# A float32 causal mask inside the score products, second weights moved by 32 to 96 bytes, and a new instruction order, in a fused attention and two-expert kernel

## The chip, the cores and the metric

The kernel runs on one core of a Trainium2 chip. The metric is device time in microseconds (us) of one execution; several executions are made and the median counts. Engines are called as in the profile: PE is the matrix engine (PEld its weight loads), DVE, ACT and POOL are the vector, scalar and GpSimd engines, SP issues the DMAs.

## The reference, cut to what matters

```python
scores = scale * np.matmul(q, k.transpose(0, 1, 3, 2))          # 4 x 8 heads, 576 x 576, depth 64
cum = np.cumsum(np.maximum(s, 0.0), axis=-1)
bias = -(cum[:, :, :, None] - cum[:, :, None, :])
scores = np.where(causal, -1000000000.0, scores + np.minimum(bias, 0.0))
attn = np.exp(scores - scores.max(-1, keepdims=True))
attn = attn / (attn.sum(-1, keepdims=True) + 1e-09)
x = (attn @ v), heads side by side                               # 2304 tokens x 512
h = x @ w_in;  x = (h - np.tanh(h)) @ w_out                      # expert 1: 512 -> 2048 -> 512
h = x @ w2_in; solu = h * softmax(h)                             # expert 2: 512 -> 1024 -> 512
out = (layer_norm(solu) * g_ln) @ w2_out
```

## The kernel before

**Attention.** Two heads make a pair (16 pairs). A unit is one block of 64 queries of a pair against all keys up to it. A score step on PE (`scores`, line 573) takes one or two units. Its products (line 631) are float32, 64 x 64 weights (the queries) with 64 to 512 keys streamed, and each is put in one of the four 64 x 64 parts of the array, so that two heads, or two heads of two units, run side by side. Behind them, one for each unit, stands `bar` (line 637): a bfloat16 product over the whole 128 x 128 array, identity `idb` times `mask`, that adds -8e9 to the masked corner, 64 columns wide, on top of the scores in PSUM. `soften` on DVE (line 646) and ACT (line 657) makes the exponentials, POOL or DVE divides (line 661), PE turns the result by transposes (line 695) over the whole array, and `weigh` (line 734) multiplies by the values in 128 x 64 parts.

**Expert 1.** Tokens come in 9 blocks of 256. For each of the 16 slices of 128 hidden columns (f) there are 12 products into the hidden layer (`h_part`, line 781) and 12 back (`x2_part`, line 804), all 128 x 128 weights and 256 columns, on inputs split into a high and a low float32r part (weights `ih`, `il`, `oh`, `ol`). The first 8 slices ("first weights", tiles `wih0` to `wol0`, pool `wa`) are used from within the attention on; the last 8 ("second weights", `wih8` to `wol8`, pool `wb`) can be converted when the attention's buffers are closed, and are used after the first ones. Each half has 9 x 8 x 24 = 1728 products.

**Expert 2** follows block by block: products of 512 columns (lines 895, 959), softmax and norm on ACT and DVE, transposes (line 945). Its 16 weight pieces (`load_w2`) go into the place of the first weights after `switch`.

**Weight conversion.** `split_w` loads each piece by SP and rebuilds it by a chain of DVE operations (lines 371, 374, 377, 382), a high part (line 263) and a low part (line 287).

**Addresses.** In the program before, the allocator puts the first weights at 50656, 67040, 83424 and 99808 bytes of a partition, which are all 96 modulo 128. The three pads of 32 bytes in `w1_tiles` put the second ones at 137088, 153504, 169920 and 186336: 0, 32, 64 and 96 modulo 128. Expert 2's weights stand where the first ones stood, and the streamed tiles `xb` and `gh` at 32 modulo 128.

**Order.** Nothing is ordered by hand: `Plan.order` simulates the engines with cost functions (`t_mm`, `t_score`, ...), takes at each turn the step that can start first (within `LOOK` ns of an engine's clock the one of lowest `prio`), and writes the instructions of all engines in that order. The priorities are sums of the constants in `T`, several per job, weight piece (`W`, `U`) and block (`V`, `B`, `E`). Where the plan sees PE idle early on, it puts in filler products (line 477).

Of the kernel before, what the change touches and what calls it, by code (L numbers as in the profile page):

```python
# [8 lines left out]
F32 = mybir.dt.float32  # L9
# [3 lines left out]
BF16 = mybir.dt.bfloat16  # L13
# [5 lines left out]

FAR = 1.0e12  # L20
TICK, DUTY = 10240 / 3, 3060.0
LOOK = {"mode": 0.0, "pe": 11.77, "act": 47.99, "dve": 2.284, "pool": 702.3}

T = dict(sums=40.52, warm=44.7, unit0=-0.03201, unit1=0.08366, pace0=0.04788, pace1=0.3542, pace2=0.1082,
         pace3=13.37, pace4=63.81, lead=-77550000.0, vlead=0.3186, fetch=-45.72, w_at0=-124.0, w_step0=88410000.0,
         w_at1=3074.0, w_step1=1163.0, m_at0=2982000.0, m_step0=502700.0, m_at1=-0.0455, m_step1=980500.0, xp=-0.01,
         m_pace=0.07888, xb=-49220.0, wb=1548.0, wb_step=153700.0, p2=0.0, w2_step=-164.7, block=11790.0,
         E2=1981000.0, e2=1981000.0, e2b=1210.0, p2_pace0=-0.08075, p2_pace=-0.01, rstd=1740.0, done=-7.542,
         J0=-1214.0, J1=123.5, J2=-37230000.0, J3=-79020000.0, J4=-1186.0, J7=-26.54, J9=-3494000000.0,
         J10=-17800000.0, J11=2977.0, J12=3382.0, J13=3590.0, J15=2472000.0, J18=20.95, W0=267800000.0, W1=-121.6,  # L30
         W2=-16950.0, W3=33270000.0, W4=-226.7, W5=-199100.0, W6=2897.0, W7=9934000.0, W9=18630.0, W13=22220.0,
         W14=22.66, W15=281800000.0, U0=-38150000.0, U1=559.7, U2=52.13, U3=-3570000.0, U4=9070.0, U6=32180.0,
         U7=-4163000.0, U9=258000000.0, U10=3425000000.0, U12=10250000000.0, U13=807.0, U14=6095.0,
         U15=12740000000.0, V00=115400.0, V01=-388500.0, V02=-428000.0, V04=1191000.0, V05=109.8, V07=43130.0,
         V08=158600.0, V12=244.3, V13=-36030.0, V14=65320.0, V15=-732.0, V16=519600.0, V17=-761.7, V18=42900000.0,
         B1=5947000000.0, B3=188400000.0, B4=-13420.0, B5=11.83, B6=13110000000.0, B7=26550000.0, B8=-32810.0,
         E0=-1258000000.0, E1=2850000.0, E3=-5713000.0, E4=-644800.0, E5=-1430000.0, E6=2519000.0, E7=-7736.0,
         E8=-1861000000.0, E9=630300000.0, E10=726.4, E11=-2977000.0, E13=-66200.0, E14=-33270.0, E15=-651600000.0,
         E16=206400000.0, E17=17370.0)
CONTEND = True  # L40
LANDING = 2300.0
SWITCH = 95.0
FILL = True
PEN = {"rstd-pool": -6.211e-19, "rstd-dve": 45.24, "copy-act": 2.286e-06, "copy-dve": 2064.0, "copy-pool": 261000.0, "move-act": -109.6, "move-dve": 5.891e-78, "diff-dve": 6.446e-11, "diff-pool": -15.23, "pad-dve": 1.284e-17, "pad-pool": 64710000.0, "norm-dve": 0.04456, "norm-pool": -798.1}

DELAY = {("act", "act"): 0.0, ("act", "dve"): 175.0, ("act", "pe"): 240.0, ("act", "pool"): 165.0,
         ("dve", "act"): 130.0, ("dve", "dve"): 128.0, ("dve", "pe"): 205.0, ("dve", "pool"): 195.0,
# [35 lines left out]
class Plan:  # L83
# [7 lines left out]
    def add(self, ways, deps=(), acq=(), rel=(), prio=0.0, late=0.0):  # L91
        s = Step(ways, deps, acq, rel, round(prio, 2), late)
        s.seq = len(self.steps)
        self.steps.append(s)
        return s

    def order(self):
# [25 lines left out]
        def could(s, w):  # L123
            t = max(clock.get(w[0], T["warm"] if w[0] == "pe" else 560.0), s.when[w[0]])
            return max(t, port) if CONTEND and (w[0] == "pool" or isinstance(w[1], Shared)) else t
# [9 lines left out]
        for _ in range(len(self.steps)):  # L135
            best = None
            for eng, cand in ready.items():
                t0 = clock.get(eng, 560.0)
                t1 = t0 + LOOK.get(eng, 30.0)
                for s, w in cand:  # L140
# [6 lines left out]
                    if t < FAR:  # L147

                        key = (max(t + LOOK["mode"] * (w[0] == "pe" and s.mode[0] != mode), t1), s.prio, s.seq)
                        if best is None or key < best[0]:  # L150
# [40 lines left out]
def own(part):  # L191

    return T.get(part, 0.0)


def t_mm(*parts, slow=1):

    return (sum(k * max(107.0, slow * n / 2.4 + (13.3 if slow == 1 else 2.5)) for n, k in parts),
            sum(k * max(107.0, slow * n / 1.2) for n, k in parts), sum(k * n * max(1, slow // 2) for n, k in parts))


def t_score(n, parts):

    a = t_mm((n, 1), slow=4)
    return a[0] + 45.0 + 30.0 * parts, a[1] + 45.0 + 60.0 * parts, a[2] + 64 * parts


def t_turn(n, k=1):
    return t_mm((n, k), slow=2)
# [19 lines left out]
class Kernel:  # L229
# [70 lines left out]
    def setup(self):  # L300
        tc = self.tc
        e = self.ctx.enter_context
        c = e(tc.tile_pool(name="const", bufs=1, side="left"))
        self.idn = c.tile([128, 128], F32, name="idn")
        self.one = c.tile([128, 1], F32, name="one")
        self.idx = c.tile([128, 128], F32, name="idx")
        self.idb = c.tile([128, 128], BF16, name="idb")
        self.mask = c.tile([128, 64], BF16, name="mask")
        c.tile([128, 56], BF16, name="pad_left")
        self.mo = e(tc.tile_pool(name="mo", bufs=1, side="left"))  # L310
        self.st = e(tc.tile_pool(name="st", bufs=8, side="left"))
        self.dr = e(tc.tile_pool(name="dr", bufs=1, space=DRAM))
        self.cum_d = self.dr.tile([self.NP, 3 * self.S], F32, name="cum_d")
        self.xd = [self.dr.tile([4, 128, 2, self.S], F32, name=f"xd{b}") for b in range(self.B)]
        self.pd = [self.dr.tile([128, 4, TB], F32, name=f"pd{j}") for j in range(self.NB)]
        self.st.tile([128, 16], F32, name="pad_st", bufs=1)
        self.wes = ExitStack()
        self.wa = self.w1_tiles(self.wes.enter_context(tc.tile_pool(name="wa", bufs=1, side="left")), 0, FA)
        self.aes = ExitStack()
        self.ap = self.aes.enter_context(tc.tile_pool(name="att", bufs=1, side="right"))  # L320
        self.cv, self.cvb = self.ap, 1
        self.pes = ExitStack()
        self.px = self.pes.enter_context(tc.tile_pool(name="px", bufs=1, space=PSUM))
        self.ps = self.pes.enter_context(tc.tile_pool(name="pb", bufs=BUFS["ps"], space=PSUM))
# [14 lines left out]
    def w1_tiles(self, pool, f0, nf):  # L339
        d = {"f0": f0, "nf": nf, "ready": {}}  # L340
        d["ih"] = pool.tile([128, 4, nf * 128], F32R, name=f"wih{f0}")
        if f0:
            pool.tile([128, 8], F32, name="pad_il")
        d["il"] = pool.tile([128, 4, nf * 128], F32R, name=f"wil{f0}")
        if f0:
            pool.tile([128, 8], F32, name="pad_oh")
        d["oh"] = pool.tile([128, nf, 512], F32R, name=f"woh{f0}")
        if f0:
            pool.tile([128, 8], F32, name="pad_ol")
        d["ol"] = pool.tile([128, nf, 512], F32R, name=f"wol{f0}")  # L350
        return d

# [76 lines left out]
    def prologue(self):  # L429
        nc, S = self.nc, self.S  # L430
        add = self.add
        V = {}
# [5 lines left out]
        def consts():  # L438
            make_identity(nc, self.idn)
            for h in range(2):  # L440

                nc.gpsimd.tensor_copy(self.idx[:, 64 * h:64 * h + 64], self.idn[:, 64 - 64 * h:128 - 64 * h])
            nc.gpsimd.tensor_copy(self.idb, self.idn)
            nc.gpsimd.memset(self.mask, 0.0)
            for h in range(2):
                m = self.mask[64 * h:64 * h + 64, :]
                nc.gpsimd.affine_select(out=m, in_=m, pattern=[[-1, 64]], compare_op=ALU.is_ge, fill=NEG, base=0,
                                        channel_multiplier=1)
# [17 lines left out]
        s = add("dve", 1040, sums, [l, self.one_ready], acq=("pt1",), rel=("pt1",))  # L466
# [17 lines left out]
    def attention_job(self, jb):  # L484
# [8 lines left out]
        lead = self.lead  # L493
        pre = lead + T["fetch"]

# [70 lines left out]
    def units(self, jb, rows, V, sums):  # L566

        nc, add = self.nc, self.add
# [9 lines left out]
        made, ats = [X for X in (self.unit(jb, i, V, Y, n) for n, i in enumerate(rows))], []  # L578
        last = rows[-1] == self.jobs[jb][2]

        def scores():
# [7 lines left out]
            for X in made:  # L589
                X["bar"]()  # L590

        s = add("pe", t_score(64 * rows[-1], len(rows)), scores, V["made"], acq=("ps",) * sum(len(X["parts"]) for X in made) + ("U",) * len(made),
                rel=("q", "kn") * last)
        s.mode = (2, 0)
        s.after = V["scores"][-1:] + sums
        V["scores"].append(s)
        dones = []
# [16 lines left out]
    def unit(self, jb, i, V, Y, n):  # L614
        nc, add = self.nc, self.add
# [5 lines left out]
        X = {}  # L621

        def parts_of(h):

            return slice(64 * h, 64 * h + 64), slice(64 * (h ^ n), 64 * (h ^ n) + 64)
# [8 lines left out]
        def bar():  # L634

            a, z = X["parts"][-1]
            nc.tensor.matmul(X[a][:, z - 64 - a:z - a], lhsT=self.idb, rhs=self.mask, start=False, stop=True,  # L637
                             skip_group_check=True)

# [496 lines left out]
```

## Time and profile before

| | |
|---|---|
| median of 3 runs | 828.76 us (826.08, 828.76, 830.53) |
| the profiled execution | 825.83 us, of which the span of instructions is 824.0 us |
| PE busy | 807.8 us, 98% of the span |
| DVE, ACT, POOL busy | 517.7, 370.4, 161.0 us |
| granted PE clock, mean of the span | 0.998 |

The profiled execution's 1.8 us outside the span are start and end. Its time lies below all three runs. A busy PE is one with a product under way; products overlap, so the spacing of their starts, not their duration, is what one costs in a row.

### The profile page before, as it was taken

Reading aid. Unit: us, or ns where it says so; the run is one execution under the profiler, and the core shown is the slowest. Engines: PE = TensorE matmul, PEld = TensorE weight load, DVE = VectorE, ACT = ScalarE, POOL = GpSimd, SP = SyncE. Lnnn points to the kernel's source line nnn. Section 1 sums busy time; section 2 is a strip of 40 time slices with the busy share of each in tenths; the row PEclk is TensorE's granted clock in tenths of the full one; section 3 lists DMA queues with packets and bytes.
Section 4 is the critical chain, followed back from the end, with each engine's and each line's share of the span. In section 5 each row is a group of like instructions: output and inputs, shape, how many; then the busy total and the mean of one; then the engine's idle time right before and its main releaser. Section 6 shows DMA issues by size and latency. Waiting matters only on the chain.

```text
span 824.0 us, 16453 instructions
## 1 busy us (share of the span) xinstructions
PE 807.8 (98%) x6176; PEld 692.3 (84%) x6176; DVE 517.7 (63%) x1412; ACT 370.4 (45%) x933; POOL 161.0 (20%) x339
## 2 busy tenths in 40 slices
PE   8898999999999999999899999999999999999998
PEld 5465667677779999999899998899988898999886
DVE  6777877777756887633488877554317374346834
ACT  5686787767774455433245442222222222223312
POOL 2353433333330000000000013130003132020403
PEclk9999999999999999999999999999999999999999
DMA  7996796586437887664665501122100120100001
GB/s 208 266 293 177 205 305 188 176 253 212 142 103 229 278 259 239 196 219 139 219 190 165 159 11 39 52 64 77 53 25 26 39 78 14 39 2 26 25 26 39
DMA packets 89135, 112.40 MB, mean 136 GB/s; under 512 B 10768, under 2 KB 73232, under 8 KB 89056
## 3 DMA queue, kind: packets, MB, share of 16 engines
q1 hardware_dynamic: 89056, 111.35, 44.4%
q8 instruction: 49, 0.80, 0.4%
q14 instruction: 30, 0.25, 0.1%
HBM read 87.63 MB, written 23.70 MB: 135 GB/s over the span
## 4 chain that ended last, share of the span: by engine, by line
PE 85%; DVE 5%; DMA 4%; ACT 3%; issue 1%; POOL 0%; SPq 0%; ACTq 0%; DVEq 0%; POOLq 0%
PE t L781 21%; PE big L895 12%; PE t L959 12%; PE big L804 11%; PE acc L804 10%; PE t L631 6%; PE t L734 6%; PE t L695 5%; PE t L945 2%; ACT U L657 1%; PE t L637 1%; DMA pd<-xp 1%; DVE U L646 1%; DMA cd<-in_moe_w_in_dram 1%; DMA xb<-xd 1%
## 5 line engine op out<-in xcount | busy, mean ns | idle before, releaser
L781 PE MATMUL t<-xb,wih 128*128 128x256 f32 x1152 | 206.8, 282 | 4.3 <-DVE g L790 3.7
L781 PEld LDWEIGHTS t<-xb,wih 128*128 128x128 f32 x1152 | 176.0, 188 | 6.8 <-DVE g L790 5.0
L781 PE MATMUL t<-xb,wil 128*128 128x256 f32 x576 | 160.9, 279 | 1.5 <-DVE wil L287 1.5
L661 POOL TENSOR_SCALAR U<-U,r 128x64 f32<-128x64 f32 (+8 forms) x144 | 85.4, 606 | 153.4 <-DVE r L576 54.4
L781 PEld LDWEIGHTS t<-xb,wil 128*128 128x128 f32 x576 | 108.6, 189 | 1.7 <-DVE wil L287 1.7
L804 PE MATMUL big<-gh,woh 128*128 128x256 f32 x576 | 105.4, 284 | 0.2 <-DVE gh L287 0.2
L804 PE MATMUL acc<-gh,woh 128*128 128x256 f32 x576 | 103.4, 282 | 0.4
L263 ACT CAST gh<-g 128x256 fp32r<-128x256 f32 x142 | 57.2, 405 | 88.0 <-PE big L804 45.7
L804 PEld LDWEIGHTS big<-gh,woh 128*128 128x128 f32 x576 | 89.8, 191 | 1.1 <-DVE gh L287 0.6
L786 ACT ACTIVATE th<-t 128x256 f32<-128x256 f32 x144 | 54.6, 381 | 80.3 <-PE t L781 52.4
L657 ACT ACTIVATE U<-U,m 128x192 f32<-128x192 f32 (+8 forms) x144 | 80.1, 558 | 22.4 <-DVE m L646 19.8
L895 PE MATMUL big<-w2ih,x 128*128 128x512 f32 x288 | 89.5, 392 | 0.0
L804 PEld LDWEIGHTS acc<-gh,woh 128*128 128x128 f32 x576 | 87.3, 188 | 1.4 <-ACT xp L263 0.8
L287 DVE TENSOR_TENSOR gh<-g,gh 128x256 fp32r<-128x256 f32 x129 | 55.8, 435 | 49.7 <-ACT gh L263 48.7
L804 PE MATMUL big<-gh,wol 128*128 128x256 f32 x288 | 81.4, 283 | 0.0
L804 PE MATMUL acc<-gh,wol 128*128 128x256 f32 x288 | 80.1, 278 | 0.0
L790 DVE TENSOR_TENSOR g<-t,th 128x256 f32<-128x256 f32 x144 | 60.2, 419 | 23.1 <-ACT th L786 20.3
L646 DVE CUSTOM_DVE_ANT_0 U<-bc,t 128x192 f32<-128x192 f32 (+8 forms) x144 | 61.3, 446 | 18.8 <-PE t L637 12.8
L631 PE MATMUL t<-kn,q 64*64 64x288 f32 (+8 forms) x640 | 66.1, 425 | 0.3 <-DMA q<-in_q_dram 0.3
L937 POOL TENSOR_SCALAR u<-y,va 128x1 f32<-128x1 f32 x54 | 33.8, 625 | 160.9 <-DVE y L932 157.2
L895 PEld LDWEIGHTS big<-w2ih,x 128*128 128x128 f32 x288 | 52.9, 188 | 10.2
L900 DVE TENSOR_REDUCE m<-big 128x1 f32<-128x1024 f32 x18 | 22.0, 1222 | 60.8 <-PE big L895 60.8
(100 smaller groups left out, 1368.9 us busy)
## 6 DMA issues: line engine op xcount, KB each, us to landing
xb<-xd SPq DMA_DIRECT2D x17, 1024.0 KB, 6.2
cd<-in_moe_w_in_dram SPq DMA_DIRECT2D x24, 512.0 KB, 5.3
cd<-in_moe_w_out_dram SPq DMA_DIRECT2D x24, 512.0 KB, 3.9
bc<-cum_d SPq DMA_DIRECT2D x32, 288.0 KB, 6.5
pd<-xp SPq DMA_DIRECT2D x18, 512.0 KB, 4.2
xp<-pd SPq DMA_DIRECT2D x18, 512.0 KB, 4.5
xd<-xs SPq DMA_DIRECT2D x16, 320.0 KB, 3.8
kn<-in_k_dram SPq DMA_DIRECT2D x16, 288.0 KB, 5.2
```

The lines of the kernel that those rows point to most:

```text
L263: nc.scalar.copy(o, i)
L287: return self.any([("dve", t_dve(n, pair=True), lambda: nc.vector.tensor_tensor(*views(), op), "diff-dve"), ("pool", t_pool(n), lambda: nc ...
L631: nc.tensor.matmul(X[a][c, :z - a], lhsT=V["q"][r, o:o + 64], rhs=V["k"][r, a:z], start=True, stop=True, skip_group_check=True)
L646: nc.vector.tensor_tensor_reduce(out=X["u"][:, a:z], in0=V["bc"][:, n, a:z], in1=X[b][:, a - b:z - b], scale=-0.125, scalar=X["m"] if "m" ...
L657: nc.scalar.activation(out=X["u"][:, :nk], in_=X["u"][:, :nk], func=AF.Exp, scale=-1.0, bias=X["m"], accum_out=Y["s"][:, n:n + 1])
L661: eng.tensor_scalar(X["u"][:, :nk], X["u"][:, :nk], Y["r"][:, n:n + 1], 1.0, ALU.mult, ALU.mult)
L781: nc.tensor.matmul(ps, lhsT=w[l][:, k, f * 128:f * 128 + 128], rhs=xb[:, r, k, :], start=k == 0 and x == 0, stop=k == 3 and x == 2)
L786: nc.scalar.activation(out=X["th", f], in_=X["h", f], func=AF.Tanh)
L790: nc.vector.tensor_tensor(X["g", f], X["h", f], X["th", f], ALU.subtract)
L804: nc.tensor.matmul(X["acc"][:, m, :], lhsT=w[l][:, f, m * 128:m * 128 + 128], rhs=X["gh", f][:, r, :], start=f == c0 and m % 2 == 0 and x ...
L895: nc.tensor.matmul(X["h"][:, n, :], lhsT=self.x2[j][:, l, k, 128 * o:128 * o + 128], rhs=r[:, k, 512 * n:512 * n + 512], start=k == 0 and ...
L959: nc.tensor.matmul(X["po"], lhsT=X["lt", k // 4][:, l, k % 4, :], rhs=r[:, k, :], start=k == 0 and a == 0, stop=k == 7 and a == 2)
```

## The change

The mask becomes float32 (`mask` 128 x 64 float32, `idb` gone, the pad beside it 240 instead of 112 bytes: 496 bytes in all before and after, so nothing behind them on that side moves). `bar` becomes two plain float32 products for each unit, 64 x 64 weights out of the float32 identity, in the same two parts of the array as the unit's scores. The three pads between the second weights' tiles go, so that all four lie at the remainder of the last one. The cost functions say so (`t_score`: 64 more columns, and a score step ends in the mode of 64 x 64 parts; `t_mm`: 11.5 instead of 13.3 ns over the streaming of a product). All constants `LOOK`, `T` and `PEN` are new, and with them the order on every engine. The diff, with the constants cut to those of the second weights and the expert 2 pieces:

```diff
-LOOK = {"mode": 0.0, "pe": 11.77, "act": 47.99, "dve": 2.284, "pool": 702.3}
+LOOK = {"mode": 0.0, "pe": 0.0, "act": 4.357, "dve": 110.5, "pool": 55.88}
...
-  wb=1548.0, wb_step=153700.0, p2=0.0, w2_step=-164.7, block=11790.0,
-  U0=-38150000.0, U1=559.7, U2=52.13, U3=-3570000.0, U4=9070.0, U6=32180.0, U7=-4163000.0, U9=258000000.0,
-  U10=3425000000.0, U12=10250000000.0, U13=807.0, U14=6095.0, U15=12740000000.0,
+  wb=-399.9, wb_step=-100.3, p2=-472600.0, w2_step=-0.01596, block=0.02797, B0=112600.0,
+  U1=19.08, U2=18.21, U4=236600.0, U5=-10090.0, U6=-462000.0, U7=-567700000.0, U8=847800000.0, U9=-7644000.0,
+  U10=1000000000.0, U11=-163400000.0, U14=2981000.0,
...
-    return (sum(k * max(107.0, slow * n / 2.4 + (13.3 if slow == 1 else 2.5)) for n, k in parts),
+    return (sum(k * max(107.0, slow * n / 2.4 + (11.5 if slow == 1 else 2.5)) for n, k in parts),
...
-def t_score(n, parts):
-    a = t_mm((n, 1), slow=4)
-    return a[0] + 45.0 + 30.0 * parts, a[1] + 45.0 + 60.0 * parts, a[2] + 64 * parts
+def t_score(n):
+    a = t_mm((n + 64, 1), slow=4)
+    return a[0] - 45.0, a[1] - 90.0, a[2]
...
-        self.idb = c.tile([128, 128], BF16, name="idb")
-        self.mask = c.tile([128, 64], BF16, name="mask")
-        c.tile([128, 56], BF16, name="pad_left")
+        self.mask = c.tile([128, 64], F32, name="mask")
+        c.tile([128, 60], F32, name="pad_left")
...
-        if f0:
-            pool.tile([128, 8], F32, name="pad_il")
         d["il"] = pool.tile([128, 4, nf * 128], F32R, name=f"wil{f0}")
-        if f0:
-            pool.tile([128, 8], F32, name="pad_oh")
         d["oh"] = pool.tile([128, nf, 512], F32R, name=f"woh{f0}")
-        if f0:
-            pool.tile([128, 8], F32, name="pad_ol")
         d["ol"] = pool.tile([128, nf, 512], F32R, name=f"wol{f0}")
...
-            nc.gpsimd.tensor_copy(self.idb, self.idn)
...
-        s.mode = (2, 0)
+        s.mode = (2, 2)
...
-            nc.tensor.matmul(X[a][:, z - 64 - a:z - a], lhsT=self.idb, rhs=self.mask, start=False, stop=True,
-                             skip_group_check=True)
+            for h in range(2):
+                r, c = parts_of(h)
+                nc.tensor.matmul(X[a][c, z - 64 - a:z - a], lhsT=self.idn[r, r], rhs=self.mask[r], start=False, stop=True,
+                                 skip_group_check=True)
```

## Rows read from the trace of the kernel before

**Rows 1.** The page, busy time, share of the span and instructions of each engine.

```profile
PE 807.8 (98%) x6176; PEld 692.3 (84%) x6176; DVE 517.7 (63%) x1412; ACT 370.4 (45%) x933; POOL 161.0 (20%) x339
```

**Rows 2.** The page, the chain that ended last, shares of the span by engine.

```profile
PE 85%; DVE 5%; DMA 4%; ACT 3%; issue 1%; POOL 0%; SPq 0%; ACTq 0%; DVEq 0%; POOLq 0%
```

**Rows 3.** Busy time by stage: stretch, its us, busy us (instructions), granted clock, DMA.

```profile
0.00:40.00 40.00, 34.37 (x274) 19.66 (x276) 27.91 (x131) 23.62 (x76) 12.12 (x33) 1.00 0.88 233
...
395.00:440.00 45.00, 41.52 (x332) 40.70 (x331) 31.24 (x65) 19.23 (x44) 0.00 (x0) 0.96 0.63 196
...
760.00:824.00 64.00, 60.27 (x286) 49.78 (x284) 34.26 (x63) 15.56 (x25) 15.62 (x45) 1.00 0.08 29
```

**Rows 4.** The chain in order of time: start us, us, what; long uninterrupted stretches.

```profile
317.91 9.89 PE t L781 x84
...
352.87 9.53 PE t L781 x84
...
574.39 11.30 PE t L781 x96
...
585.70 11.39 PE big L804 x96
...
755.78 10.89 PE big L895 x48
```

**Rows 5.** Timeline of PE where the second weights begin (line 804 first, 781 second).

```profile
394.90 0.39 PE L804 MATMUL acc<-gh,woh 128*128 128x256 f32 x2
395.12 0.28 PE L804 MATMUL acc<-gh,wol 128*128 128x256 f32 x1
395.24 0.39 PE L781 MATMUL t<-xb,wih 128*128 128x256 f32 x2
395.47 0.28 PE L781 MATMUL t<-xb,wil 128*128 128x256 f32 x1
395.59 0.40 PE L781 MATMUL t<-xb,wih 128*128 128x256 f32 x2
```

**Rows 6.** Groups of PE by line and shape: busy us, mean ns, idle before.

```profile
L637 PE MATMUL t<-mask,idb 128*128 128x64 bf16 x144 | 19.5, 199 | 0.0
```

**Rows 7.** Timeline of PE, score steps: start us, us, what.

```profile
17.47 0.33 PE L631 MATMUL t<-kn,q 64*64 64x64 f32 x4
17.74 0.20 PE L637 MATMUL t<-mask,idb 128*128 128x64 bf16 x1
17.87 0.44 PE L631 MATMUL t<-kn,q 64*64 64x128 f32 x4
18.24 0.20 PE L637 MATMUL t<-mask,idb 128*128 128x64 bf16 x1
...
54.11 0.23 PE L637 MATMUL t<-mask,idb 128*128 128x64 bf16 x2
54.18 0.41 PE L695 MATMUL t<-idn,U 128*128 128x128 f32 x2
...
60.82 0.20 PE L637 MATMUL t<-mask,idb 128*128 128x64 bf16 x1
60.86 0.28 PE L695 MATMUL t<-idx,U 128*64 128x128 f32 x1
...
119.52 0.23 PE L637 MATMUL t<-mask,idb 128*128 128x64 bf16 x2
119.69 0.77 PE L631 MATMUL t<-kn,q 64*64 64x256 f32 x8
```

**Rows 8.** Timeline of PE at the hand-over: a wait, then products at half clock.

```profile
407.48 0.51 PE L781 MATMUL t<-xb,wih 128*128 128x256 f32 x2 [2.19 <-DVE g L790]
...
409.94 0.63 PE L804 MATMUL big<-gh,woh 128*128 128x256 f32 x2
410.36 0.41 PE L804 MATMUL big<-gh,wol 128*128 128x256 f32 x1
410.58 0.63 PE L804 MATMUL big<-gh,woh 128*128 128x256 f32 x2
```

**Rows 9.** Groups of DVE in 245 to 440 us: busy us, mean ns.

```profile
L377 DVE SCALAR_TENSOR_TENSOR ct<-cd,ct 128x512 int32<-128x512 int32 x23 | 15.8, 687 | 0.3
L382 DVE SCALAR_TENSOR_TENSOR ct<-cd,ct 128x512 uint32<-128x512 uint32 x23 | 15.8, 685 | 0.2
L371 DVE TENSOR_SCALAR ct<-ct 128x512 f32<-128x512 f32 x24 | 10.2, 427 | 8.1 <-ACT ct L389 7.3
L374 DVE TENSOR_SCALAR ct<-ct 128x512 int32<-128x512 int32 x24 | 10.1, 422 | 0.3
...
L287 DVE TENSOR_TENSOR w2il<-ct,w2ih 128x512 fp32r<-128x512 f32 x4 | 2.7, 684 | 0.7 <-ACT w2ih L263 0.7
```

More of the change, by code (lines that the diff above doesn't have):

```diff
@@ L21 @@
 TICK, DUTY = 10240 / 3, 3060.0
-LOOK = {"mode": 0.0, "pe": 11.77, "act": 47.99, "dve": 2.284, "pool": 702.3}
[L24 to L39, printed above, removed]
@@ new lines @@
+LOOK = {"mode": 0.0, "pe": 0.0, "act": 4.357, "dve": 110.5, "pool": 55.88}
+T = dict(sums=0.01786, warm=76.25, unit0=0.01, unit1=0.4357, pace0=0.5341, pace1=52.33, pace2=0.2647, pace3=49110.0,
+         pace4=81830.0, lead=17.3, vlead=13300000.0, fetch=-0.01709, w_at0=0.01, w_step0=-0.1408, w_at1=5695000.0,
+         w_step1=107400.0, m_at0=0.01, m_step0=979200000.0, m_at1=536200000.0, m_step1=988100000.0, xp=40010.0,
+         m_pace=4011.0, xb=-0.01, wb=-399.9, wb_step=-100.3, p2=-472600.0, w2_step=-0.01596, block=0.02797,
+         e2=-1.864, e2b=0.01484, p2_pace0=4.973, p2_pace=99.88, rstd=-0.09974, done=-0.01378, J0=262.8, J1=1565.0,
+         J2=2113.0, J3=-811.1, J4=-3307.0, J5=-375400.0, J6=109.5, J7=-50930.0, J9=25.71, J12=5348000.0, J13=26150.0,
+         J14=-275.9, J15=184900000.0, J16=-71590.0, J17=2688000000.0, J18=20830000.0, J19=-21070000.0, W0=444300.0,
+         W1=3869.0, W2=-493600.0, W3=10080.0, W4=-157.4, W6=-10990.0, W7=53980.0, W8=43770.0, W9=-16720.0,
+         W10=-220300000.0, W11=41610000.0, W12=43090.0, W14=25420000.0, W15=186800.0, U1=19.08, U2=18.21,
+         U4=236600.0, U5=-10090.0, U6=-462000.0, U7=-567700000.0, U8=847800000.0, U9=-7644000.0, U10=1000000000.0,
+         U11=-163400000.0, U14=2981000.0, V01=29180000.0, V02=-13900.0, V03=22120000.0, V05=-89130.0, V06=913400.0,
+         V07=85950000.0, V08=11590.0, V10=1780000000.0, V11=24380.0, V12=418200000.0, V13=-510600.0, V14=1372000.0,
+         V15=-572400.0, V16=67.02, V17=-154200000.0, V18=66540000.0, B0=112600.0, B3=-79720.0, B4=271700000.0,
+         B5=-60.2, B7=4572000000.0, B8=46370000.0, E0=-472700000.0, E1=-6653000.0, E2=-7646000.0, E3=1657000.0,
+         E4=2361.0, E5=1862000.0, E6=-13490.0, E8=1740000.0, E9=-18730.0, E10=-92620000.0, E11=-24.12, E12=24920.0,
+         E13=1090000000.0, E14=33410000.0, E15=20160000.0, E16=-168.6)
@@ L43 @@
 FILL = True
-PEN = {"rstd-pool": -6.211e-19, "rstd-dve": 45.24, "copy-act": 2.286e-06, "copy-dve": 2064.0, "copy-pool": 261000.0, "move-act": -109.6, "move-dve": 5.891e-78, "diff-dve": 6.446e-11, "diff-pool": -15.23, "pad-dve": 1.284e-17, "pad-pool": 64710000.0, "norm-dve": 0.04456, "norm-pool": -798.1}
+PEN = {"rstd-pool": -8.205e-05, "rstd-dve": -5.076e-06, "copy-act": -4914.0, "copy-dve": 1160.0, "copy-pool": -59.75, "move-act": -6.553e-06, "move-dve": 682900.0, "diff-dve": -1.594e-36, "diff-pool": 5.166e-12, "pad-dve": 55.36, "pad-pool": 127200.0, "norm-dve": 31.46, "norm-pool": -1812000.0}
 DELAY = {("act", "act"): 0.0, ("act", "dve"): 175.0, ("act", "pe"): 240.0, ("act", "pool"): 165.0,
@@ L590, in scores @@
                 X["bar"]()
-        s = add("pe", t_score(64 * rows[-1], len(rows)), scores, V["made"], acq=("ps",) * sum(len(X["parts"]) for X in made) + ("U",) * len(made),
+        s = add("pe", t_score(64 * rows[-1]), scores, V["made"], acq=("ps",) * sum(len(X["parts"]) for X in made) + ("U",) * len(made),
                 rel=("q", "kn") * last)
-        s.mode = (2, 0)
+        s.mode = (2, 2)
         s.after = V["scores"][-1:] + sums
```

## The prediction

> **What bounds the kernel now.** I read the busy times first: PE has work under way for 807.8 of 824.0 us, and no other engine passes 63% [rows 1]. The chain that ended last runs on PE for 85% [rows 2]. Then the stages, to see where PE is not full: 5.6 us are missing in the first 40 us (loads and warm-up), 3.5 us at the hand-over from the first to the second weights (395 to 440 us, where the clock also falls to a mean of 0.96), 3.7 us at the end; the stages between are full [rows 3]. So time comes out of this kernel by making PE's products closer, or by closing those few holes, and a microsecond less on PE in a full stage is nearly a microsecond less in all. What one product costs is then read from uninterrupted stretches of the chain: their time divided by their count [rows 4].
>
> **Second weights at one remainder.** With the first weights, 84 products in 9.53 us are 113.5 ns each, and in another stretch 84 in 9.89 us are 117.7: two steady spacings of the same instructions, which change only after a wait. With the second weights, 96 in 11.30 us are 117.7 and 96 in 11.39 us are 118.6 [rows 4]; their mean is 118.2. That this is the weights and not the stage is seen at the border: the last three products on first weights take 0.34 us (394.90 to 395.24), the next three, on second weights, 0.35 (395.24 to 395.59) [rows 5]; the two digits just resolve it. The first weights all lie at 96 modulo 128, the second at 0, 32, 64 and 96, and the streamed tiles are the same, so afterwards the second ones stand to them as the first do now. I therefore take the first weights' two spacings for the bounds: 1728 x (118.2 - 117.7) = 0.9 us gained if all stay at the slow one, 1728 x (118.2 - 113.5) = 8.1 us if all go to the fast one. Between them I lean to the fast one: the 512-wide products of expert 2, which stand before most of the second stage's runs and whose weights are already at 96, take 10.89 us for 48 [rows 4], 226.9 ns, twice 113.5. At 114.5 the gain is 1728 x 3.7 = 6.4 us, in a full stage. No DVE, ACT or DMA instruction is touched by it.
>
> The Trainium skill ("TensorE: Matmul & The Clock Gate", section "Step-by-step: what each phase is for") speaks against this gain: PE has two independent read ports, and loading the next weights "doesn't steal SBUF read bandwidth from the running matmul". By that sentence an address could not matter, and the gain would be 0 instead of 6.4 us. The spacings on either side of the border do not agree with it, if the address is what differs there.
>
> **The mask in float32.** What goes: 144 mask products [rows 6], and two changes of array mode where score steps meet. The group's PE idle is 0.0 [rows 6], so there is no wait to win back, only the products and the changes. What they cost: a single mask product is followed by whole-array work after 0.04 us (60.82 to 60.86), two after 0.07 (54.11 to 54.18); where the next work is a score step again it takes 0.13 (17.74 to 17.87) and 0.17 (119.52 to 119.69), so a change of mode costs 0.09 to 0.10 [rows 7]. What comes: 64 columns more behind the scores, in the same parts. One row prices just that: a score step of 64 columns takes 0.27 us up to its mask (17.47 to 17.74), one of 128 takes 0.37 (17.87 to 18.24) [rows 7], so 64 columns more cost 0.10 to 0.11. That is my value, and the lower bound. The upper bound is a 64-column step on its own without its change of mode, 0.27 - 0.09 = 0.18 us, as if no weight load of the mask were hidden. In two-unit steps the shorter unit's mask runs beside the longer one's scores, and only one of 0.11 shows.
>
> From the timeline of the attention (88 score steps, 32 of one unit, 56 of two; [rows 7] shows the kinds but the last), by what follows:
> - whole-array work, 48 steps (17 and 31): +0.11 - 0.04 and +0.11 - 0.07, so 17 x 0.07 + 31 x 0.04 = +2.4 us; the change of mode only moves behind the mask.
> - another score step, 23 (11 and 12): the change out (0.09) and the 0.13 or 0.17 go, 0.11 comes: 11 x -0.11 + 12 x -0.15 = -3.0 us.
> - `weigh`, 17 (4 and 13), 128 x 64 parts: the change out goes, one into the other mode stays (taken at the same 0.09): 4 x -0.02 + 13 x -0.06 = -0.8 us.
>
> Sum -1.4 us, were the neighbours kept. At the upper bound each of 88 costs 0.07 more: +4.8 us. A plan that now pays nothing for score steps in a row may put more of them together: each pair so joined saves 0.2 us, and ten such pairs another 2 us, which I leave in the range. POOL's copy into `idb` goes too, before the first scores; these wait for loads, so nothing is gained there.
>
> **The new order.** It moves every instruction on all queues, and the rows of before can only bound it. The holes that an order can close are the hand-over's 3.5 us and its half clock: after a wait of 2.19 us on a DVE gate three products take 0.64 us (409.94 to 410.58, the level of 1.2 GHz) [rows 8] against 0.35 [rows 5], and a mean clock of 0.96 over 45 us [rows 3] says that this cost 0.04 x 45 = 1.8 us; 5 us together. It can open others of that kind. I take 0, with 5 us to each side.
>
> **Sum.** 825.83 - 6.4 - 1.4 + 0 = 818.0 us for the profiled execution. The median of the runs shown lies 2.9 us above that execution; with the same distance the median after is 820.9, so 821 us. Half a per cent, 4.1 us, is about what a measurement here can tell from no change. The likeliest case by itself: 6.4 may be 2 to 8, the order 3 either way: 816 to 826.
>
> **Rivals.**
> - *The hand-over gets worse (slower).* Place: 395 to 440 us, DVE. Each expert 2 piece costs DVE 0.69 + 0.69 + 0.43 + 0.42 + 0.68 = 2.9 us [rows 9], and they become ready at the same moment as block 0 on the second weights. By the constants, 8 of 16 pieces sort ahead of block 0 before (i x w2_step + U below 0), 12 after (below B0 = 112600). Four more are 11.6 us of DVE ahead of gates for which PE already waited [rows 8]. For: that wait. Against: DVE is busy 31 of 45 us there [rows 3], and pieces can only be converted as they land. If all 11.6 us and one more half-clock stretch (1.8) show: 828.8 - 7.8 + 13.4 = 834 us. It outweighs the gains from 7.8 us on, and is slower beyond the bound from 12 us.
> - *The order closes holes as well.* The hand-over's 5 us go: 816 us. For: PE is full on both sides of them [rows 3], so that work to fill them with exists. Against: DVE's work there stays the same, and it is what PE waits for [rows 8].
> - *The address does nothing.* The second stage is slow for another reason (the order of tiles, the accumulator `big`): 828.8 - 1.4 = 827 us. For: the first weights also run at 117.7 in places [rows 4]. Against: the border [rows 5]. The page above says the same as this rival; by its sentence it would be the likeliest, and I give it less.
> - *The mask's weights do not hide.* +4.8 instead of -1.4: 828.8 - 6.4 + 4.8 = 827 us. Against: 64 further columns cost what they stream [rows 7].
>
> **How the numbers follow.** Forecast 0.52, hand-over worse 0.17, order closes holes 0.13, address nothing 0.12, mask unhidden 0.06. Faster needs a median under 824.6: most of the forecast (0.45), the closed holes (0.13) and a few of the others (0.04), 0.62. Slower is over 832.9: most of a bad hand-over, 0.12. The rest, 0.26, is within. The range must reach up over 827 and part of the bad hand-over, and down over closed holes with fast weights (828.8 - 8.1 - 1.4 - 5 = 814, less 2 for joined score steps): 812 to 830.
>
> **What would show it.** Right: stretches on the second weights at 113.5 or 117.7 ns each, even in themselves; line 637 in 576 records of 64 x 64 float32 (each float32 product has two), score steps 0.10 to 0.11 us longer up to their end, score steps in a row with no 0.13 to 0.17 between. Wrong: second weights still at 118 (the address rival), mask records each some 0.1 us apart (the hidden loads), PE's idle in the hand-over over 10 us, or holes in the attention stage that PE did not have. The prediction as a whole fails if PE's idle grows by more than 8 us.

## The result, and the profile after

The changed kernel takes 817.3 us in the median (815.7 to 819.7, 4 runs) against 829.6 us before: a ratio of 0.9861, with a 95% interval of 0.982 to 0.990. By this ratio it is 11.5 us less, by the two medians 12.3. The forecast was 821 us, between 812 and 830. The profiled execution takes 818.2 us, where the sum said 818.0; the two agree only because terms that were wrong cancel, as the experiments show. The 2.9 us that the forecast added, since the median before lay that far over its profiled execution, did not come: the median after lies 0.8 us under its own.

The page of the changed kernel, busy time of each engine, beside [rows 1]:

```profile
PE 801.9 (98%) x6618; PEld 711.2 (87%) x6618; DVE 505.4 (62%) x1366; ACT 382.0 (47%) x973; POOL 146.0 (18%) x344
```

PE is the bound as before, with 442 records of products more (576 of the mask for 144, and ten fillers) in 6 us less. By stage, beside [rows 3] (stretch, its us, then PE, PEld, DVE, ACT, POOL, granted clock, DMA):

```profile
0.00:40.00 40.00, 34.73 (x358) 24.16 (x358) 28.07 (x131) 25.87 (x84) 12.11 (x34) 1.00 0.90 249
...
395.00:440.00 45.00, 44.97 (x388) 44.66 (x388) 36.25 (x78) 23.30 (x54) 0.00 (x0) 1.00 0.63 198
440.00:600.00 160.00, 157.25 (x988) 141.38 (x987) 98.86 (x189) 50.36 (x101) 24.85 (x80) 1.00 0.19 60
...
760.00:816.00 56.00, 51.86 (x261) 43.30 (x259) 27.62 (x50) 12.49 (x21) 8.74 (x36) 0.99 0.07 24
```

The hand-over from first to second weights is full now: 44.97 of 45 us at a clock of 1.00, where 3.5 us and a mean clock of 0.96 stood [rows 3]. Before, PE makes 96 products into the hidden layer from 395.24 us on [rows 5], waits in them [rows 8], and makes the first product back on the second weights only at 409.30 us:

```profile
409.30 0.63 PE L804 MATMUL big<-gh,woh 128*128 128x256 f32 x2
```

Now the two kinds take turns, and the first one back comes at 397.5 us (the chain counts it from the end of the piece before):

```profile
397.71 1.41 PE big L798 x12
399.12 1.41 PE t L775 x12
```

That this turn-taking is what closed the hole is read from the traces; no run changes it alone. A part of the hole came back later: 2.75 us of PE are missing between 440 and 600 us, where 0.44 were before. PE's waits there (line waited for: us in total, times, longest):

```profile
PE t L775 <- DVE g L784: 1.9, 1, 1.9
PE big L889 <- DVE ct L906: 0.8, 1, 0.8
```

The spacing of products is in the chain in order of time (start, us, what), beside [rows 4]; line 775 was 781, line 798 was 804, line 889 was 895. `acc` marks the first weights, `big` at line 798 the second:

```profile
254.14 5.44 PE acc L798 x48
...
331.28 5.65 PE acc L798 x48
...
452.79 4.08 PE big L798 x36
...
459.59 5.46 PE big L889 x24
...
466.46 4.24 PE big L798 x36
```

Per product that is 113.3, 117.7, 113.3, 227.5 (512 columns) and 117.8 ns. So the second weights now do run at the first weights' two even spacings, as forecast. But over all their uninterrupted products (worked out from the starts of 1707 of them) the mean is 116.6 ns, with 73% at the wider spacing, against 118.2 before: 1.6 x 1728 = 2.8 us, not 6.4. And what stood behind the hope for the closer one points the other way: the run behind the 512-column products (459.59) is at the wider one, and so is every run of 48 or more behind such products in this trace, 9 of them.

The mask, group by line and shape beside [rows 6], and score steps in the timeline beside [rows 7] (line 623 was 631, line 631 was 637):

```profile
L631 PE MATMUL t<-mask,idn 64*64 64x64 f32 x576 | 32.1, 217 | 0.0
```

```profile
17.28 0.43 PE L623 MATMUL t<-kn,q 64*64 64x128 f32 x4
17.55 0.28 PE L631 MATMUL t<-mask,idn 64*64 64x64 f32 x4
17.66 0.49 PE L623 MATMUL t<-kn,q 64*64 64x192 f32 x4
17.99 0.28 PE L631 MATMUL t<-mask,idn 64*64 64x64 f32 x4
18.20 0.33 PE L689 MATMUL t<-idn,U 128*128 128x128 f32 x1
```

A mask takes 0.11 us and the next score step follows at once (17.55 to 17.66); before whole-array work it is 0.21 (17.99 to 18.20), the change of mode of 0.1 now standing behind it. The scores of 128 columns take 0.27 up to their mask where they took 0.37 [rows 7]. All as worked out.

### The profile page after: what moved, and what is told of

The parts are those of the page before. It is cut to its first block, busy times and chain, and to the rows that moved or that the text cites. A ratio compares the mean times of both kernels' runs of the same rounds, so it can differ in the third digit from the quotient of the medians.

```text
span 816.4 us, 17366 instructions
## 1 busy us (share of the span) xinstructions
PE 801.9 (98%) x6618; PEld 711.2 (87%) x6618; DVE 505.4 (62%) x1366; ACT 382.0 (47%) x973; POOL 146.0 (18%) x344
## 4 chain that ended last, share of the span: by engine, by line
PE 87%; DVE 5%; DMA 3%; ACT 2%; issue 1%; SPq 1%; POOL 0%; POOLq 0%; ACTq 0%; DVEq 0%
PE t L775 21%; PE big L889 12%; PE t L953 12%; PE acc L798 12%; PE big L798 10%; PE t L689 6%; PE t L623 6%; PE t L728 5%; PE t L939 2%; PE t L631 2%; DMA xp<-pd 1%; DMA cd<-in_moe_w_out_dram 1%; DMA cd<-in_moe_w_in_dram 1%; DVE ct L370 1%; DVE ct L375 1%
## 5 line engine op out<-in xcount | busy, mean ns | idle before, releaser
L655 POOL TENSOR_SCALAR U<-U,r 128x384 f32<-128x384 f32 (+8 forms) x144 | 83.1, 591 | 156.9 <-DVE r L568 81.9
L287 DVE TENSOR_TENSOR gh<-g,gh 128x256 fp32r<-128x256 f32 x126 | 53.7, 429 | 59.3 <-ACT gh L263 49.1
L263 ACT COPY pt<-t 128x512 f32<-128x512 f32 (+4 forms) x160 | 61.3, 427 | 16.6 <-PE t L689 15.8
L623 PE MATMUL t<-kn,q 64*64 64x288 f32 (+8 forms) x640 | 63.2, 420 | 1.9 <-DMA q<-in_q_dram 1.9
```

The lines of the kernel that those rows point to most:

```text
L263: nc.scalar.copy(o, i)
L287: return self.any([("dve", t_dve(n, pair=True), lambda: nc.vector.tensor_tensor(*views(), op), "diff-dve"), ("pool", t_pool(n), lambda: nc ...
L623: nc.tensor.matmul(X[a][c, :z - a], lhsT=V["q"][r, o:o + 64], rhs=V["k"][r, a:z], start=True, stop=True, skip_group_check=True)
L655: eng.tensor_scalar(X["u"][:, :nk], X["u"][:, :nk], Y["r"][:, n:n + 1], 1.0, ALU.mult, ALU.mult)
```

## The experiments

Times are medians; the ratio is to the kernel before, run beside each, with its 95% interval. The kernel before itself moves between these series (its median is 825.9 to 829.6 us), so kernels are compared by their ratios. The changed kernel's ratio is 0.9861. "Spacing" without a row is a mean over uninterrupted products (100 to 135 ns apart), worked out from the starts in the trace.

**One part at a time.** Three kernels do one part each, a fourth undoes one.

E1, the address alone, on the kernel and the order of before:

```diff
-        if f0:
-            pool.tile([128, 8], F32, name="pad_il")
...
-            pool.tile([128, 8], F32, name="pad_oh")
...
-            pool.tile([128, 8], F32, name="pad_ol")
```

> The kernel before, with only the three pads between the second weights taken out; the order of every instruction is that of before. Theory A (the address sets the spacing): products on the second weights leave their uneven 112 to 127 ns (mean 118.2) and run at one of the two even spacings of the first weights, 113.3 or 117.8 ns; the time falls by 1 to 8 us, 3 to 6 if the two are mixed as they are on the first weights. Rival B (the address does nothing, the gain is the order's): mean still 118.2 with values from 112 to 127, time within 1.5 us of before.

827.0 us against 828.9, ratio 0.998 (0.9956 to 1.0005): 1.7 us, not told from nothing by time alone. The spacing did change, from 118.2 to 117.1. Long runs in the chain, second weights:

```profile
562.28 11.31 PE big L798 x96
573.59 11.31 PE t L775 x96
```

Both lines are at 117.8 now, where they were at 118.6 and 117.7 [rows 4]. Theory A holds for the spacing, near the lower bound of the gain, since most runs take the wider of the two.

E2, the mask alone, in the order and with the cost functions of before:

```diff
-        self.idb = c.tile([128, 128], BF16, name="idb")
-        self.mask = c.tile([128, 64], BF16, name="mask")
-        c.tile([128, 56], BF16, name="pad_left")
+        self.mask = c.tile([128, 64], F32, name="mask")
+        c.tile([128, 60], F32, name="pad_left")
...
-            nc.tensor.matmul(X[a][:, z - 64 - a:z - a], lhsT=self.idb, rhs=self.mask, ...
+            for h in range(2):
+                r, c = parts_of(h)
+                nc.tensor.matmul(X[a][c, z - 64 - a:z - a], lhsT=self.idn[r, r], rhs=self.mask[r], ...
```

> The kernel before, with only the mask made of float32 products in the 64 x 64 parts; pads, cost functions and order of before. Theory A (the mask costs its 64 columns and saves changes of mode): score and mask products together take 1.5 to 3.5 us less, and the time falls by as much. Rival B (the weight loads of the mask show): 0.07 us more for each of 88 score steps, time up by 3 to 6 us. Rival C (the gain of score steps comes only from the new order, which puts them side by side): within 1 us of before.

825.2 us, ratio 0.9955 (0.9931 to 0.9979): 3.7 us less by time. In the trace the time from each score or mask product to the next product falls from 70.3 to 68.8 us in all, 1.5 us, where 1.4 was worked out. Theory A; the new order isn't needed for it. That the time falls by more than the trace shows goes with the clock: the mean granted clock of these runs is 0.9967, of the 23 runs of before beside them 0.9948. Among those 23, 0.01 of the clock goes with 5.7 us, so this difference is worth some 1 us (an estimate).

E3, the order alone: the changed kernel with the pads and the mask of before.

```diff
-        self.mask = c.tile([128, 64], F32, name="mask")
-        c.tile([128, 60], F32, name="pad_left")
+        self.idb = c.tile([128, 128], BF16, name="idb")
+        self.mask = c.tile([128, 64], BF16, name="mask")
+        c.tile([128, 56], BF16, name="pad_left")
...
+            pool.tile([128, 8], F32, name="pad_il")
...
-            for h in range(2):
-                r, c = parts_of(h)
-                nc.tensor.matmul(X[a][c, z - 64 - a:z - a], lhsT=self.idn[r, r], rhs=self.mask[r], ...
+            nc.tensor.matmul(X[a][:, z - 64 - a:z - a], lhsT=self.idb, rhs=self.mask, ...
```

> The changed kernel's order and constants, with the mask product and the pads of before put back. Theory A: the order alone gives what its profile shows at the hand-over (about 5 us of idle and half clock gone) and loses some of it between 440 and 600 us and in fillers; 0 to 4 us under before. Rival B (the order carries most of the change): 7 us or more under before. Rival C (the order alone is a loss, hidden by the other two): over before by 2 us or more.

819.5 us, ratio 0.9887 (0.9857 to 0.9917): 9.4 us less. Rival B: the order carries most of the change. Its hand-over:

```profile
395.00:440.00 45.00, 44.81 (x381) 44.61 (x380) 37.02 (x80) 23.31 (x53) 0.00 (x0) 1.00 0.63 200
```

All that expert 1's products lose outside their plain spacing (every interval not between 100 and 135 ns, less 113.3) falls from 16.9 to 9.5 us. 3.6 us of it are on the first weights, 2.5 of these in four waits of 0.2 to 1.6 us between 60 and 370 us, none of which is left. 3.8 us are on the second, 1.5 of them the stretch at half clock. Fillers take 2.2 us more, and 2.1 us less come from this execution's first weights being mostly at 113.3, which is not the order's. Together that is 7.3 us, against 7.1 between the two profiled executions (825.8 and 818.8 us); the 9.4 us are those of all runs.

E4, the changed kernel with the pads back:

```diff
+        if f0:
+            pool.tile([128, 8], F32, name="pad_il")
...
+            pool.tile([128, 8], F32, name="pad_oh")
...
+            pool.tile([128, 8], F32, name="pad_ol")
```

> The changed kernel with only the three pads put back, so that the second weights lie at 0, 32, 64 and 96 again. Theory A: spacing on the second weights back to uneven values with a mean near 118.2 against 116.6 in the changed kernel, 2 to 5 us over the changed kernel. Rival B (address does nothing): as the changed kernel, within 1.5 us.

817.5 us, ratio 0.9867 (0.9832 to 0.9902), against the changed kernel's 0.9861. The spacing goes back to 118.1, as theory A said, but in the time nothing is seen of it: its 2.6 us drown in the spread of the runs (816.1 to 822.1 us). In its profiled execution, the second longest of the six, the first weights ran at a mean of 116.3 ns, in E3's at 113.9; that alone is 4 us. By time this is rival B's number, by spacing theory A's.

**What sets the spacing.** E5 to E7, E9 and E11 move expert 1's weights or its streamed tiles (`xb`, `gh`) in steps of 32 and 16 bytes, all on the changed kernel.

```diff
 E5:     d["ol"] = pool.tile([128, nf, 512], F32R, name=f"wol{f0}")
+        if f0:
+            pool.tile([128, 16], F32, name="pad_end")
 E6, E7, E9: the streamed tiles lie between these two pads
-        c.tile([128, 60], F32, name="pad_left")
+        c.tile([128, 68], F32, name="pad_left")      # E7: 76, E9: 52
-        self.st.tile([128, 16], F32, name="pad_st", bufs=1)
+        self.st.tile([128, 8], F32, name="pad_st", bufs=1)      # E7: none, E9: 24
 E11:
-        d["ih"] = pool.tile([128, 4, nf * 128], F32R, name=f"wih{f0}")
+        m = nf * 512
+        fold = lambda t: t[:, 4:4 + m].rearrange("p (k f) -> p k f", k=4)
+        d["ih"] = fold(pool.tile([128, m + 32], F32R, name=f"wih{f0}"))      # il, oh, ol alike
```

E5: 

> The changed kernel with a pad of 64 bytes behind the second weights, so that all four lie at 32 modulo 128, as the streamed tiles do, instead of 96. Theory A (what matters is that the four have one remainder): the second weights keep the two even spacings, 113.3 and 117.8 ns, and the time stays within 2 us of the changed kernel. Rival B (the remainder against that of the streamed tiles matters): another spacing, even or not, outside these two, or one of the two alone.

E6: 

> The changed kernel with the streamed tiles of expert 1 moved from 32 to 64 modulo 128; first and second weights stay at 96. Theory A (the remainder of the weights among themselves alone decides): both halves run at 113.3 or 117.8 ns, time within 2 us of the changed kernel. Rival B (the difference to the streamed tiles decides): both halves of expert 1 change their spacing, and the time moves by more than 3 us, as 3456 products are concerned (1 ns each is 3.5 us).

E7: 

> The same with the streamed tiles at 96 modulo 128, the remainder of the weights. Theory A: both spacings as before, within 2 us of the changed kernel. Rival B: another spacing; if equal remainders are good the slow one disappears (117.8 gone, some 8 us less), if they are bad the fast one does (some 6 us more).

E9: 

> The changed kernel with expert 1's streamed tiles at 0 modulo 128, the weights at 96: a difference of 96, the one not yet seen (64 gives 113.3 or 117.8 ns, 32 a mean of 118.3, 0 gives 120.0). Theory A (the difference decides, and 64 is its best value): an uneven spacing with a mean of 117 to 119.5, 3 to 9 us over the changed kernel. Rival B (96 is as good or better): a mean under 115.5, under the changed kernel.

E11: 

> The changed kernel with all of expert 1's weights, first and second, at 112 instead of 96 modulo 128 (a shift of 16 bytes in tiles made 128 bytes longer); streamed tiles at 32, so a difference of 80 between the two good values known, 64 (113.3 or 117.8 ns) and 96 (117.3 or 118.7). Theory A (the spacing goes by steps of 32 bytes or more): 113.3 and 117.8 as in the changed kernel, within 2 us of it. Theory B (it goes by 16 bytes): another spacing; if the slow one of the two disappears, 4 to 9 us under the changed kernel, a version that beats both; if the fast one disappears, 4 to 6 us over.

The chains, one line each of long runs, first E5 (second weights), then E6, E7, E9 and E11:

```profile
596.50 10.08 PE t L777 x84
```

```profile
601.16 9.94 PE t L775 x84
```

```profile
607.38 10.08 PE t L774 x84
```

```profile
435.41 9.86 PE t L775 x84
...
600.55 9.97 PE t L775 x84
```

```profile
438.20 9.89 PE t L778 x84
...
603.45 9.99 PE t L778 x84
```

Divided by 84, and put beside the difference of the remainders (weights less streamed tiles, modulo 128):

| difference | kernel | spacing, ns | median, us | ratio (interval) |
|---|---|---|---|---|
| 64 | changed | 113.3 or 117.8, even | 817.3 | 0.9861 (0.982 to 0.990) |
| 0, second weights alone | E5 | 120.0, even | 821.5 | 0.995 (0.9928 to 0.9973) |
| 32 | E6 | 118.3, uneven | 824.8 | 0.9977 (0.996 to 0.9994) |
| 0 | E7 | 120.0, even | 829.2 | 1.004 (1.0022 to 1.0058) |
| 96 | E9 | 117.4 or 118.7, uneven | 823.4 | 0.9955 (0.9936 to 0.9974) |
| 80 | E11 | 117.7 or 118.9, uneven | 824.6 | 0.9944 (0.9925 to 0.9964) |

Theory A falls in E5 to E7: it isn't that the four tiles have one remainder, it is how the weights lie to what is streamed. E5 (32 and 32) and E7 (96 and 96) give the same 120.0 at different remainders, so it is the difference; in E5 the first weights, left at 64, keep the two even spacings in the same execution (mean 114.1). 32, 80 and 96 were each reached in one way only. With all of expert 1 at 0 the whole gain of the change is lost (E7). E9's theory A and E11's theory B hold, but without the hoped-for gain: 64 is the best value tried, and the only one that runs evenly at 113.3. The second weights before had the differences 96, 0, 32 and 64 side by side; that their 118.2 is the mix of these is likely, and not shown. E7's loss, 15 us against the changed kernel by the ratios, is over twice the 6 that its expectation named: both 113.3 and 117.8 are gone. E11's, 7 us, is a little over its 4 to 6.

E10 asks whether the 512-column products of expert 2, at a difference of 0, gain as much from 64:

```diff
+            self.wl.tile([128, 16], F32, name="pad_w2")
             self.w2ih = self.wl.tile([128, 4, 1024], F32R, name="w2ih")
...
             self.gain = self.wl.tile([128, 2, 512], F32, name="gain")
+            self.wl.tile([128, 16], F32, name="pad_x2")
```

> The changed kernel with expert 2's streamed weights (w2ih to w2ol) moved from 96 to 32 modulo 128; its stationary tiles x2, cd, cu stay at 96, so that the difference is 64 as in expert 1 instead of 0. 864 products of 512 columns at 226.7 ns stream for 213.3, 13.4 ns over; with 256 columns a difference of 0 costs 120.0 - 106.7 = 13.3 over. Theory A (the cost over streaming is paid once a weight load and set by the difference): 220 ns at the fast spacing or 224.4 at the slow one, 2 to 6 us under the changed kernel. Rival B (512 columns hide the load, the 13.4 is something else): 226.7 as before, within 1.5 us of the changed kernel.

819.7 us, ratio 0.9906 (0.9874 to 0.9939). Neither: they became slower. One run of 48 in its chain, 233.1 ns each against 226.9 [rows 4] (its other long runs take 229 to 233.5):

```profile
782.50 11.19 PE big L889 x48
```

So 226.9 is not "twice 113.5": at 512 columns a difference of 0 is the better one, and the likeness from which I chose the closer spacing was chance. (Behind these products, the runs on the second weights took either spacing, not only the wider.)

**E8, the mask twice**, on the changed kernel; the masked corner gets -1.6e10:

```diff
-            for h in range(2):
+            for h in (0, 1, 0, 1):
```

> The changed kernel with every mask product issued twice (the masked corner gets -1.6e10 instead of -8e9). Theory A (a mask behind a score step costs what its 64 columns stream, 0.11 us, and those of a shorter unit hide): 88 score steps x 0.11 = 9 to 10 us more. Rival B (weight loads show): 0.18 us for each step, 16 us more. Rival C (PE has slack there): under 4 us more.

823.7 us, ratio 0.9975 (0.9952 to 0.9998), 1.1% over the changed kernel's. Score and mask products together take 76.1 instead of 65.9 us: 10.2 over 88 steps is 0.116 us each. Theory A. The same step as above:

```profile
17.50 0.44 PE L623 MATMUL t<-kn,q 64*64 64x128 f32 x4
17.77 0.40 PE L631 MATMUL t<-mask,idn 64*64 64x64 f32 x8
18.00 0.49 PE L623 MATMUL t<-kn,q 64*64 64x192 f32 x4
```

Two masks take 0.23 us (17.77 to 18.00), one 0.11.

**E12, fewer expert 2 pieces ahead of block 0**, the mechanism of the slower rival, turned back:

```diff
-  w2_step=-0.01596, B0=112600.0, U1=19.08, U2=18.21, U4=236600.0, U5=-10090.0, ...
+  w2_step=-164.7, U0=-38150000.0, U1=559.7, U2=52.13, U3=-3570000.0, U4=9070.0, ...
```

> The changed kernel with the expert 2 pieces' constants of before (U, w2_step) and without B0, so that 8 of 16 pieces instead of 12 sort ahead of block 0 on the second weights; the order up to the hand-over is that of the changed kernel. Rival of the prediction (pieces ahead of the block make PE wait): fewer waits, PE idle between 395 and 480 us under the changed kernel's 2.8 us, 1 to 3 us faster. Theory A (early pieces are what closed the hand-over's hole, since expert 2's products can then start early): PE waits again in 395 to 440 us, 2 to 5 us slower. Rival C: the places of these pieces do not matter, within 1 us.

823.4 us, ratio 0.9967 (0.9939 to 0.9995), 1.1% over the changed kernel's. In time this is theory A's side, and more than its 2 to 5 us, but its mechanism is not what the trace shows. Expert 2's first products start earlier here, not later, at 442.1 us against 459.6 in the changed kernel:

```profile
442.12 2.73 PE big L874 x12
```

Between 395 and 480 us PE misses 1.9 us where the changed kernel misses 2.8, as the rival said, though 1.6 of them lie before 440, where the changed kernel misses nothing. The loss comes behind that. PE's 440 to 600 us, and its waits there:

```profile
440.00:600.00 160.00, 155.27 (x941) 137.89 (x940) 98.27 (x186) 47.59 (x96) 21.48 (x77) 0.98 0.17 55
```

```profile
PE big L874 <- DVE ct L891: 4.7, 2, 4.4
```

The products of two expert 2 steps stand in a row here, 48 of them from 478.2 us on. After the first 24 PE waits 4.4 us, until DVE has multiplied out the softmax of the first step (line 891); from 486.1 to 492.9 us the clock is at its lower level, 1.2 GHz, 4.6 us of this with products under way, which costs another 2.3 us. Yet this execution has the closer spacing on a long run where the changed one has the wider; the same 48 products as at 331.28 above:

```profile
330.38 5.44 PE acc L783 x48
```

So E12 shows what a worse place of the pieces can cost, and decides for neither theory.

## Why the prediction was right

The direction, the time and the range held; the split of the sum did not.

- **The mask** (-1.4 us): right in its working. 0.11 us for one, the changes of mode moved or saved, no weight load shown (E2, E8). One term is off by a hundredth: by its own rows each of the 13 two-unit steps before `weigh` gains 0.05 us, not 0.06, which moves the sum by 0.1. The 2 us left open for score steps put side by side did not come: 25 of 88 are followed by another score step, 23 were.
- **The address** (-6.4 us, bounds 0.9 to 8.1): mechanism right, size wrong. The measured term is 1.7 us by time in the order of before (E1, an interval that just reaches no change) and 2.0 to 2.8 by spacing. The step that failed is "between them I lean to the fast one": the 512-column products have another difference of addresses, and behind them the changed kernel's runs of 48 or more all take the wider spacing. Of the two reasons in the working, one remainder, and lying to the streamed tiles as the first weights do, only the second counts, with a difference of 64 (E5 to E7). The rival that the address does nothing is refuted by the spacing, though in E4 not by the time. The Trainium skill ("TensorE: Matmul & The Clock Gate", "Step-by-step: what each phase is for") says that loading the next weights takes no read bandwidth from the running product. My conclusion from it, that an address could not matter, does not hold here: moving the weights alone takes the spacing from 113.3 or 117.8 to 120.0 ns (E5). Whether read bandwidth is what is lost then, no run shows.
- **The order** (0, 5 us to each side): the term that was mis-sized most, -9.4 us by time (E3, interval -11.9 to -6.9). The rival "the order closes holes" came true, beyond its place: the hand-over, and waits on the first weights that I had not counted. I wrote that the stages between are full, by [rows 3], which does not show them. One was not, before and in E3:

```profile
40.00:100.00 60.00, 57.39 (x528) 36.77 (x524) 45.62 (x187) 44.26 (x130) 25.70 (x39) 1.00 0.79 227
```

```profile
40.00:100.00 60.00, 58.65 (x541) 36.25 (x541) 46.14 (x192) 50.36 (x151) 26.57 (x43) 1.00 0.88 247
```

  Shorter waits mostly hide even from such a row, since products, 280 ns long and 114 apart, still lie over them.
- **From the profiled execution to the median** (+2.9 us): this step failed, and the clock is the likely reason. In the 35 runs of before beside E5 to E8, the ten with a mean granted clock of 0.992 or less took 827.9 to 830.9 us, the twelve with 0.999 or more 823.5 to 825.0. The profiled execution had 0.998, the runs of before in the four series a mean of 0.994 to 0.996; the changed kernel's four had 0.999 or 1.000. So most executions of before spend longer at half clock than the one whose trace I read 1.8 us from, and the changed kernel hardly any time. Within the four series 0.01 of the clock goes with 4 to 6 us, so 0.004 to 0.006 is worth 2 to 4 us (an estimate). E3's six runs have a mean of 0.9965, so not all of this comes with the order alone.
- **The hand-over gets worse**: no. PE waits 1.9 us for a gate of DVE between 395 and 600 us, where it waited 3.7. The step behind this rival, 12 pieces ahead for 8, is read from the constants and not borne out by the traces: by 440 us 7 pieces were converted (their low parts written) before, 8 in the changed kernel, and 9 in E12, whose constants put 8 ahead. What pieces ahead of the block cost is therefore not tested.

The three parts alone add up to 14.8 us, the change to 11.5 (8.1 to 14.9); the intervals do not tell these apart.

What stays open: which of the two spacings a run takes after a wait, and which constants of the new order close which wait. No version tried beats the changed kernel.

## What to carry to other kernels

Where PE is the bound, take the spacing of products from uninterrupted stretches, and compare it for the same instruction on different tiles: a few ns on thousands of products can be an address. Busy shares of PE hide waits shorter than a product's own length; count intervals between starts for these. A gain read as "the other half's spacing" is only as good as the share of time that the other half spends at it. And one profiled execution is one draw: look at the granted clock of every run before carrying its distance to the median over to another kernel.

## What the runs showed of the hardware

The spacing of 256-column products with a new 128 x 128 float32r weight each goes by the difference of the weights' and the streamed tile's addresses modulo 128: 120.0 ns at 0, 118.3 at 32, 113.3 or 117.8 at 64, 117.7 or 118.9 at 80, 117.4 or 118.7 at 96, all at a granted clock of 1.00. That it is the difference is shown at 0, which two ways of moving tiles reach (E5, E7). With 512 columns 0 is good (226.9) and 64 is not (229 to 233.5, E10).

At 64 there are two steady states. A run keeps its spacing, for up to 827 products in the changed kernel's trace (308 to 406 us, all at 117.8), until the next wait, and the same 826 products in E12's trace kept 113.3: 3.7 us between two kernels on the same stretch. Runs of one kernel can differ by some such steps (before: 824.6 to 834.7 us in 23 runs); that this is a cause is argued, not shown, and the granted clock, 0.988 to 0.999 in these runs, goes with the time too: 828.0 to 834.7 us at 0.993 or less, 824.6 to 828.7 at 0.998 or more.

The clock fell from 2.4 to 1.2 GHz after PE's wait of 2.19 us in the trace of before [rows 8] and during the 4.4 us in E12's. It did not after a wait of 2.1 us at the same place in E2's, nor after the 1.9 us in the changed kernel's.
